# Rounding g behind its leaky step, ordering the head's first chunks by unit, and storing the last tokens by 64 columns

## The chip, the cores and the metric

The kernel runs on one core of a Trainium2 chip. Its engines work side by side, each through a queue of its own in order: TensorE (PE in the profile; its weight loads are PEld), VectorE (DVE), ScalarE (ACT), GpSimd (POOL) and SyncE (SP), which only issues DMAs here. Sixteen DMA engines move data. The metric is device time of one execution in microseconds (us).

## What is computed

```python
# attention over 32 memory slots: q, k, v (8, 8, 576, 64), phi (8, 8, 576, 32)
a = exp(phi - max(phi, axis=2)); a = a / (sum(a, axis=2) + 1e-9)
k_m = einsum('bhsm,bhsd->bhmd', a, k); v_m = einsum('bhsm,bhsd->bhmd', a, v)
scores = q @ k_m^T / 8; attn = softmax(scores)          # over the 32 slots
x = attn @ v_m                                          # (4608 tokens, 512)
# first layer
h = x @ w_in                                            # 512 -> 2048
g = maximum(0.01 * h, h)                                # the leaky step
x2 = g @ w_out                                          # 2048 -> 512
# second layer
gate = 1 / (1 + exp(-(x2 @ w_gate))); val = x2 @ w_val  # 512 -> 1536
out = (gate * val) @ w2_out                             # 1536 -> 512
```

All of it is float32. Where TensorE multiplies, the kernel writes each operand as a rounded part ("hi") and the remainder ("lo") and adds three products: hi by hi, lo by hi, hi by lo. Making the two parts, `split`, is a ScalarE cast and a subtraction on VectorE or GpSimd.

## The kernel before

**Attention and first layer.** The work goes by batch b (8), and within it by unit (b, g): g is one of two groups of four heads. A unit's chain is cut into parts: `v...` parts run on VectorE, ScalarE and GpSimd, `t...` parts on TensorE. `v10` ends the softmax, `v10t` transposes the result, `v11` splits it into `at_hi` and `at_lo`, one half of the tokens (288) after the other. x is never made: `vw` holds v_m times a block of 256 columns of w_in, per unit (`vw_block` for batch 0, `vw_pair` after), split like the rest, and h comes from `at` and `vw`.

The first layer goes by steps, one for each batch, token half `hf` and chunk `fc` of 128 of the 2048 columns (256 steps; in batch 0, groups of four chunks for one half, then for the other). A step has two parts. `m1_in` (line 845) makes h of the chunk in a bank of PSUM (`ps_h`, two banks): six products of 288 columns, three for unit g = 0 and then three for g = 1; then ScalarE's leaky step into `gr` (line 861); it hands back a function that splits `gr` into `gh` and `gl` (`ghl`). `m1_out` (line 868) adds the chunk's share of x2 to four banks `acc`: for each of four column blocks wh by gh, wl by gh, wh by gl. At a batch's end (in batch 0 at a group's end) `acc` is copied or added to `obuf` or `pbuf` and stored.

The loop over the steps (line 1373) has all engines' orders written out by hand. `LA` is 2: in iteration i come, in this order,

```python
            if fin:
                fin()                          # split of g of step i + 1
                fin = None
            if i + LA < len(steps):
                fin = step_in(*steps[i + LA])  # h and leaky step of step i + 2
```

then the other work of the iteration (units' parts, the conversion of weights by `tick`, later the preparation of the second layer's weights by `stash`, finished `vw` blocks), then `m1_out` of step i. A `tick` moves the weight pieces of w_in and w_out on by a stage each: ScalarE's `a` (y, k and the raw words), VectorE's `b` and `b2`, GpSimd's `c`, and the split `d` (ScalarE's cast of `wo`, GpSimd's subtraction). The list `gldve` names six steps whose subtraction of g is VectorE's; the others are GpSimd's.

Ahead of the loop stands the prologue, a list of groups of parts; within a group the chains of the units and of the ticks are run in turns, one piece of each in a round. After it `vw` blocks 0 and 1 are computed and split (chunks 0 and 1 need block 0, chunk 2 block 1), and `step_in` is called for steps 0 and 1.

**Second layer.** It goes by five pairs of token blocks, `PAIRS`, each of 2 h tokens, h being 512 or 384; the last has 384. Products of 2 x 2 blocks are made with seven products in place of eight. `m2_out` adds the seven products of the output weights, in the order k = 0, 2, 1, 5, 4, 3, 6, each in two column halves e, from four banks to `sums[j]`, j = 2 q + t (t: token block, q: column part); a `sum` is finished with k = 5 (j = 1), 4 (j = 3), 3 (j = 0), 6 (j = 2). `sums` hold columns on partitions, so VectorE transposes them, 32 x 32 blocks, into a tile `turned` and DMAs write rows of `out`. `turn` puts a transpose on the list `lazy`; each `read` (the VectorE or ScalarE instruction that empties a bank) takes `turns` entries from it. In the last pair's last `m2_out` (`last and end`) two entries are taken per addition, tokens are transposed by 256 and by 128, and a token block is stored when all its 512 columns have been turned: four DMAs for each of the two chunks, in pieces of 128 columns (512 B), from SyncE's and ScalarE's queues by turns.

Of the kernel before, what the change touches and what calls it, by code (L numbers as in the profile page):

```python
# [26 lines left out]
 'ticks': [1, 1, 1, 1, 2, 1, 1, 2, 0, 1, 0, 1, 1, 2, 0, 0, 0, 1, 1, 1, 1, 1, 0, 0, 1, 0, 0, 0, 0, 0],  # L27
# [95 lines left out]
def tile_kernel(  # L123
# [720 lines left out]

    def m1_in(b, hf, fc):
        p = ps_h.tile([P, 512], F32, tag="h", name="ps_h")
        t = vw[b, fc * P // VB]
        o = (fc * P) % VB
        n = 0
        for g in range(NG):  # L850
            wh, wl = t[:, 0, g, o:o + P], t[:, 1, g, o:o + P]
            i = at[b, hf, g]
            ah, al = at_hi[:, i, :], at_lo[:, i, :]
            if fc == NF - 1:
                at_free.append(i)
            for w, x in ((wh, ah), (wl, ah), (wh, al)):
                nc.tensor.matmul(p[:, :HALF], w, x, start=(n == 0), stop=(n == 3 * NG - 1))  # L857
                n += 1
        gh, gl = ghl_next()
        gr = gr_next()  # L860
# [280 lines left out]
    def m2_out(n, th, between):  # L1141
# [9 lines left out]
        def stored(t, x, m, st):  # L1151
            f = lazy.pop()
            lazy.append(lambda: (f(), store(t0 + t * h + x, m, st, end)))

        chunks = [(0, 256), (256, h - 256)]
        st = {}
        for k, e in OUT_SEQ:
# [14 lines left out]
            if th == 0 and k in (0, 2, 1, 6):  # L1172
                read(lambda: nc.scalar.copy(o, b), turns=1)
            else:
                read(lambda: nc.vector.tensor_add(o, b, o), turns=2 if end and last else 1)  # L1175
            for f in between.pop(0) if between else ():
                f()
            if last and end and (j := {5: 1, 4: 3, 3: 0, 6: 2}.get(k)) is not None:
                t = j % 2
                for x, m in chunks:  # L1180
                    if (t, x) not in st:
                        st[t, x] = turned()
                    turn(j, e, x, m, st[t, x])
                    if (k, e) in ((4, 1), (6, 1)):
                        stored(t, x, m, st[t, x])
            elif last and not end and (k, e) in ((4, 1), (6, 1)):
                t = k == 4
                for x, m in chunks:
# [4 lines left out]
                    stored(t, x, m, o)  # L1193
        while last and end and lazy:
            lazy.pop(0)()

    n_st = [0]
# [4 lines left out]

    def store(n0, m, o, end):
        for g in range(4):
            (nc.scalar if end and g % 2 else nc.sync).dma_start(
                out=out[n0:n0 + m, P * g:P * g + P].rearrange("(b p) d -> p b d", p=32),
# [4 lines left out]
    with tc.manual_schedule():  # L1211
# [114 lines left out]
        waiting = []  # L1326
        n_vw = n_in = 0
        fin = None
        for group in SCHED["prologue"]:
# [24 lines left out]
        while n_vw < 2:  # L1354
            run([first_vw(n_vw)()])
            n_vw += 1
        for i in range(LA):
            fin = step_in(*steps[i])
            if i + 1 < LA:
                fin()  # L1360

# [11 lines left out]
        for i, (b, hf, fc) in enumerate(steps):  # L1373
            if fin:
                fin()
                fin = None
            if i + LA < len(steps):
                fin = step_in(*steps[i + LA])
            else:
# [39 lines left out]
        for n in range(len(PAIRS)):  # L1419
# [25 lines left out]
            m2_out(n, NTH - 1, between)  # L1445
            if n + 2 == len(PAIRS):
                for _ in range(2):
                    t = p2[0].tile([P, 2 * PC], F32, tag="xr", name="turned", bufs=7)
                    stage2.append(t.rearrange("p (b q r) -> p b q r", q=4, r=32))

# [29 lines left out]
```

## Time and profile before

| | us |
|---|---|
| median of three runs | 1563.75 |
| lowest and highest | 1563.34 and 1563.9 |
| the profiled execution | 1563.91 |
| its span, from the first to the last instruction | 1562.1 |
| TensorE busy | 1513.7 |
| VectorE, ScalarE, GpSimd busy | 949.9, 818.4, 455.2 |

The times in the rows below are those of the profiled execution, counted from the start of its span. "Idle before" is the time in which an engine had no work ahead of an instruction, with what ended it.

### The profile page before, as it was taken

How to read it: one execution, taken by the hardware profiler on the slowest of the kernel's cores; microseconds unless marked ns; L12 is line 12 of the kernel's file. 1: busy time of each engine (PE TensorE's matmuls, PEld its weight loads, DVE VectorE, ACT ScalarE, POOL GpSimd, SP SyncE). 2: the span in 40 equal slices, each digit the busy share in tenths (PEclk: the TensorE clock that was granted, in tenths of full speed). 3: DMA queues.
4: the chain of work that ended last, by engine and by line, in shares of the span. 5: the costliest groups of instructions: out<-in, count | busy, mean ns of one | idle time of the engine just before them, and what ended most of it. 6: DMA issues, size and time to landing. Idle time of an engine off the chain costs nothing.

```text
span 1562.1 us, 28982 instructions
## 1 busy us (share of the span) xinstructions
PE 1513.7 (97%) x10508; PEld 1357.9 (87%) x10508; DVE 949.9 (61%) x1732; ACT 818.4 (52%) x1846; POOL 455.2 (29%) x445
## 2 busy tenths in 40 slices
PE   5788999999999999999999999999999999999997
PEld 2677999999999999999999988888888888889997
DVE  6886555556655555522066665757666865668567
ACT  5885565666566565644444454534532544435432
POOL 2986364554545445533200030004000210003000
PEclk9999999999999999999999999999999999999999
DMA  9822664555556555411398887667866687668875
GB/s 303 294 54 59 166 178 135 179 153 167 167 167 188 153 177 160 128 53 60 100 320 261 246 236 248 194 193 216 274 195 193 189 247 234 194 193 235 295 250 156
DMA packets 278094, 297.11 MB, mean 190 GB/s; under 512 B 102080, under 2 KB 176320, under 8 KB 277952
## 3 DMA queue, kind: packets, MB, share of 16 engines
q1 hardware_dynamic: 276288, 294.47, 63.0%
q8 instruction: 84, 1.38, 0.4%
q10 hardware_dynamic: 1664, 0.79, 0.2%
q14 instruction: 58, 0.48, 0.1%
HBM read 243.27 MB, written 51.90 MB: 189 GB/s over the span
## 4 chain that ended last, share of the span: by engine, by line
PE 79%; DVE 4%; ACT 1%; POOL 1%; issue 1%; DMA 0%; DVEq 0%; SPq 0%; ACTq 0%; POOLq 0%
PE acc L880 21%; PE ps_y L1030 18%; PE oacc L1165 13%; PE ps_h L857 10%; PE ps_z L1030 9%; PE ps_x L1030 5%; PE ps_vw L827 2%; DVE op L1046 1%; DVE sum L1175 1%; PE ps_kv L593 1%; POOL xo L953 1%; DVE sg L1049 1%; PE ps_sc L668 0%; DVE sg L1055 0%; DVE tmp L1058 0%
## 5 line engine op out<-in xcount | busy, mean ns | idle before, releaser
L880 PE MATMUL acc<-ghl,wo 128*128 128x288 f32 x3072 | 461.4, 299 | 7.3 <-ACT obuf L889 2.6
L880 PEld LDWEIGHTS acc<-ghl,wo 128*128 128x128 f32 x3072 | 420.3, 188 | 32.8 <-issue 10.7
L1030 PE MATMUL ps_y<-xo,wt 128*128 128x512 f32 (+1 forms) x1440 | 328.8, 368 | 0.0
L189 POOL TENSOR_TENSOR ghl<-grs,ghl 128x288 fp32r<-128x288 f32 x250 | 217.7, 873 | 317.7 <-ACT ghl L188 239.7
L1030 PEld LDWEIGHTS ps_y<-xo,wt 128*128 128x128 f32 x1440 | 262.5, 188 | 36.1 <-ACT tmp L1061 2.0
L1165 PE MATMUL oacc<-op,wt 128*128 128x512 f32 (+1 forms) x1260 | 265.1, 369 | 1.4 <-DVE sum L1175 0.5
L1165 PEld LDWEIGHTS oacc<-op,wt 128*128 128x128 f32 x1260 | 228.3, 188 | 35.8 <-DVE sum L1175 4.5
L861 ACT ACTIVATE grs<-ps_h 128x288 f32<-128x288 f32 x256 | 105.4, 412 | 248.7 <-PE ps_h L857 227.0
L1061 ACT COPY tmp<-ps_y 128x512 f32<-128x512 f32 (+1 forms) x180 | 98.0, 544 | 256.8 <-PE ps_y L1030 256.7
L857 PE MATMUL ps_h<-at_hi,vw 128*128 128x288 f32 x1024 | 214.1, 297 | 3.6 <-ACT vw L188 2.7
L953 POOL TENSOR_TENSOR xo<-xr,xo 128x512 fp32r<-128x512 f32 (+1 forms) x28 | 39.4, 1436 | 598.0 <-ACT xo L949 598.0
L857 PEld LDWEIGHTS ps_h<-at_hi,vw 128*128 128x128 f32 x1024 | 166.2, 190 | 5.0 <-ACT vw L188 3.6
L1030 PE MATMUL ps_z<-xo,wt 128*128 128x512 f32 (+1 forms) x720 | 167.6, 367 | 0.3 <-POOL xo L953 0.3
L1175 DVE TENSOR_TENSOR sum<-oacc,sum 128x512 f32<-128x512 f32 (+1 forms) x170 | 106.5, 633 | 89.9 <-PE oacc L1165 89.1
L857 PE MATMUL ps_h<-at_lo,vw 128*128 128x288 f32 x512 | 151.8, 297 | 0.0
L1030 PEld LDWEIGHTS ps_z<-xo,wt 128*128 128x128 f32 x720 | 131.7, 188 | 17.5 <-POOL xo L953 0.7
L1058 DVE TENSOR_TENSOR tmp<-ps_x,tmp 128x512 f32<-128x512 f32 (+1 forms) x60 | 38.0, 633 | 177.8 <-PE ps_x L1030 177.8
L1042 ACT CAST op<-sg 128x512 fp32r<-128x512 f32 (+1 forms) x180 | 103.4, 579 | 76.3 <-DVE sg L1049 47.5
L188 ACT CAST ghl<-grs 128x288 fp32r<-128x288 f32 x256 | 111.7, 436 | 1.9
L1046 DVE TENSOR_TENSOR op<-sg,op 128x512 fp32r<-128x512 f32 (+1 forms) x180 | 111.9, 645 | 0.5
L857 PEld LDWEIGHTS ps_h<-at_lo,vw 128*128 128x128 f32 x512 | 97.2, 190 | 0.0
L839 DVE TENSOR_TENSOR vw<-ps_vw,vw 128x256 fp32r<-128x256 f32 x112 | 39.7, 416 | 81.8 <-ACT vw L837 81.8
(177 smaller groups left out, 1750.0 us busy)
## 6 DMA issues: line engine op xcount, KB each, us to landing
wt<-gvs SPq DMA_DIRECT2D x420, 256.0 KB, 3.0
wt<-w2s SPq DMA_DIRECT2D x210, 256.0 KB, 3.0
gvs<-hl SPq DMA_DIRECT2D x60, 256.0 KB, 2.6
x2s<-obuf SPq DMA_DIRECT2D x15, 576.0 KB, 3.4
win<-in_moe_w_in_dram SPq DMA_DIRECT2D x16, 512.0 KB, 9.7
wo_bits<-in_moe_w_out_dram SPq DMA_DIRECT2D x16, 512.0 KB, 10.5
q<-in_q_dram SPq DMA_DIRECT2D x224, 36.0 KB, 3.0
w2s<-hl SPq DMA_DIRECT2D x30, 256.0 KB, 2.4
```

The lines of the kernel that those rows point to most:

```text
L188: nc.scalar.copy(hi, raw)
L189: eng.tensor_sub(lo, raw, f32(hi))
L857: nc.tensor.matmul(p[:, :HALF], w, x, start=(n == 0), stop=(n == 3 * NG - 1))
L861: nc.scalar.activation(gr, p[:, :HALF], AF.Prelu, alpha=0.01)
L880: nc.tensor.matmul(a[d][:, :HALF], w[:, d * P:(d + 1) * P], x, start=(open_ and n == 0), stop=(close and n == 2),)
L953: eng.tensor_sub(t[:, 1, :h], x_operand(n, k, a), f32(t[:, 0, :h]))
L1030: nc.tensor.matmul(bank, w[:, l, a, :], x[:, r, :h], start=(start and i == 0), stop=(i == 5), skip_group_check=not start,)
L1042: return lambda: nc.scalar.copy(ops[j][k][:, 0, :h], x)
L1046: return lambda: nc.vector.tensor_sub(t[:, 1, :h], x, f32(t[:, 0, :h]))
L1061: return lambda: nc.scalar.copy(d, x)
L1165: nc.tensor.matmul(b, w[:, j, l, :], ops[j][k][:, r, :h], start=(start and i == 0), stop=(i == 5), skip_group_check=not start,)
L1175: read(lambda: nc.vector.tensor_add(o, b, o), turns=2 if end and last else 1)
```

## The change

Four things are changed, and the arithmetic stays.

- In the loop, the split of a step's g is issued directly behind its leaky step, in iteration i for step i + 2, ahead of the iteration's other work; it was issued in iteration i + 1.
- The prologue's last group gets the part `v0.1`, which computes `vw` block 0 and splits it between `v10.1` and `v10t.1`; block 1 stays behind the prologue.
- Steps 0 and 1 are begun with the three products of unit 0 for both chunks; then follow the three of unit 1, leaky step and split for one chunk after the other.
- In the last pair's last `m2_out` each finished column half is transposed at once, 384 tokens in one instruction, ahead of the next addition. After the second half of a j, four DMAs store 64 columns (256 B) of 384 tokens for each group of 32 partitions. The tiles `turned` of this pair lie where `at_hi` and `at_lo`, later the second layer's `tmp`, lay, and the two further `turned` tiles of the pair before fall away. `store` of the other pairs issues from SyncE's queue alone, as it did for them.

```diff
--- before.py
+++ after.py
@@ -23,7 +23,7 @@
  'prologue': ['v1.0', 't1.0', 'v2.0 t7a.0 t2.0', 'v7a.0 v3.0', 'v3e.0 v4.0', 't7b.0 v1.1', 'T t4.0 t1.1', 'T',
               'v5.0', 'v7b.0', 'v2.1', 't5.0', 'v6.0 t2.1 t8a.0', 'T v3.1', 'v3e.1 v8a.0 t8b.0', 't7a.1', 'v8b.0',
               'v9.0 v7a.1 T v4.1 v9e.0 t4.1', 't7b.1 T', 't5.1 v5.1 v7b.1', 'T', 'v10.0 T', 't8a.1 v6.1',
-              'v10t.0 t8b.1 T v8a.1', 'v11.0', 'v8b.1 v9.1 T', 'T T v9e.1 T v10.1 v10t.1 v11.1'],
+              'v10t.0 t8b.1 T v8a.1', 'v11.0', 'v8b.1 v9.1 T', 'T T v9e.1 T v10.1 v0.1 v10t.1 v11.1'],
  'ticks': [1, 1, 1, 1, 2, 1, 1, 2, 0, 1, 0, 1, 1, 2, 0, 0, 0, 1, 1, 1, 1, 1, 0, 0, 1, 0, 0, 0, 0, 0],
  'banks': 9,
  'lopool': [0, 1, 2, 3, 4, 5, 6, 7, 8, 9, 10, 11, 12, 13, 14],
@@ -842,12 +842,12 @@
     gt = {}
     acc = {}
 
-    def m1_in(b, hf, fc):
-        p = ps_h.tile([P, 512], F32, tag="h", name="ps_h")
+    def m1_in(b, hf, fc, begun=None, gs=range(NG)):
+        p = begun or ps_h.tile([P, 512], F32, tag="h", name="ps_h")
         t = vw[b, fc * P // VB]
         o = (fc * P) % VB
-        n = 0
-        for g in range(NG):
+        n = 3 * gs[0]
+        for g in gs:
             wh, wl = t[:, 0, g, o:o + P], t[:, 1, g, o:o + P]
             i = at[b, hf, g]
             ah, al = at_hi[:, i, :], at_lo[:, i, :]
@@ -856,6 +856,8 @@
             for w, x in ((wh, ah), (wl, ah), (wh, al)):
                 nc.tensor.matmul(p[:, :HALF], w, x, start=(n == 0), stop=(n == 3 * NG - 1))
                 n += 1
+        if gs[-1] < NG - 1:
+            return p
         gh, gl = ghl_next()
         gr = gr_next()
         nc.scalar.activation(gr, p[:, :HALF], AF.Prelu, alpha=0.01)
@@ -1150,7 +1152,7 @@
 
         def stored(t, x, m, st):
             f = lazy.pop()
-            lazy.append(lambda: (f(), store(t0 + t * h + x, m, st, end)))
+            lazy.append(lambda: (f(), store(t0 + t * h + x, m, st)))
 
         chunks = [(0, 256), (256, h - 256)]
         st = {}
@@ -1172,17 +1174,23 @@
             if th == 0 and k in (0, 2, 1, 6):
                 read(lambda: nc.scalar.copy(o, b), turns=1)
             else:
-                read(lambda: nc.vector.tensor_add(o, b, o), turns=2 if end and last else 1)
+                read(lambda: nc.vector.tensor_add(o, b, o), turns=1)
             for f in between.pop(0) if between else ():
                 f()
             if last and end and (j := {5: 1, 4: 3, 3: 0, 6: 2}.get(k)) is not None:
                 t = j % 2
-                for x, m in chunks:
-                    if (t, x) not in st:
-                        st[t, x] = turned()
-                    turn(j, e, x, m, st[t, x])
-                    if (k, e) in ((4, 1), (6, 1)):
-                        stored(t, x, m, st[t, x])
+                if t not in st:
+                    st[t] = gp.tile([P, 1536], F32, tag="at_hi" if t else "at_lo", name="turned", bufs=1)
+                    st[t] = st[t].rearrange("p (b q r) -> p b q r", q=4, r=32)
+                turn(j, e, 0, h, st[t])
+                lazy.pop()()
+                if e:
+                    f = 64 * (j // 2)
+                    for g in range(4):
+                        (nc.scalar if g % 2 else nc.sync).dma_start(
+                            out=out[t0 + t * h:t0 + t * h + h, P * g + f:P * g + f + 64].rearrange("(b p) d -> p b d", p=32),
+                            in_=st[t][32 * g:32 * g + 32, :, j - t:j - t + 2].rearrange("p b q r -> p b (q r)"),
+                        )
             elif last and not end and (k, e) in ((4, 1), (6, 1)):
                 t = k == 4
                 for x, m in chunks:
@@ -1191,18 +1199,15 @@
                         for e2 in range(2):
                             turn(j, e2, x, m, o)
                     stored(t, x, m, o)
-        while last and end and lazy:
-            lazy.pop(0)()
-
     n_st = [0]
 
     def turned():
         n_st[0] += 1
         return stage2[n_st[0] % len(stage2)]
 
-    def store(n0, m, o, end):
+    def store(n0, m, o):
         for g in range(4):
-            (nc.scalar if end and g % 2 else nc.sync).dma_start(
+            nc.sync.dma_start(
                 out=out[n0:n0 + m, P * g:P * g + P].rearrange("(b p) d -> p b d", p=32),
                 in_=o[32 * g:32 * g + 32, 0:m // 32].rearrange("p b q r -> p b (q r)"),
             )
@@ -1324,8 +1329,8 @@
             else:
                 (unit_phi, unit_kv, unit_q)["pkq".index(x[0])](units[int(x[1])])
         waiting = []
-        n_vw = n_in = 0
-        fin = None
+        n_vw = 1
+        PARTS["v0"] = lambda u: first_vw(0)()
         for group in SCHED["prologue"]:
             vs, ts_ = {}, []
             for n, f in enumerate(waiting):
@@ -1354,10 +1359,9 @@
         while n_vw < 2:
             run([first_vw(n_vw)()])
             n_vw += 1
+        begun = [m1_in(*steps[i], None, (0,)) for i in range(LA)]
         for i in range(LA):
-            fin = step_in(*steps[i])
-            if i + 1 < LA:
-                fin()
+            m1_in(*steps[i], begun[i], (1,))()
 
         early = {0: [(x_open, ())] + [(x_load, (0, c)) for c in range(KD)]}
         for n in range(8):
@@ -1371,11 +1375,8 @@
         first = m2_group(0, 0, 0, 0)
         held = None
         for i, (b, hf, fc) in enumerate(steps):
-            if fin:
-                fin()
-                fin = None
             if i + LA < len(steps):
-                fin = step_in(*steps[i + LA])
+                step_in(*steps[i + LA])()
             else:
                 if not tmps:
                     tmp_open()
@@ -1443,10 +1444,6 @@
                         eng = nc.vector if len(todo) < 3 else nc.gpsimd
                         between[-1] += [lambda o=o: x_hi(*o), lambda o=o, eng=eng: x_lo(*o, eng)]
             m2_out(n, NTH - 1, between)
-            if n + 2 == len(PAIRS):
-                for _ in range(2):
-                    t = p2[0].tile([P, 2 * PC], F32, tag="xr", name="turned", bufs=7)
-                    stage2.append(t.rearrange("p (b q r) -> p b q r", q=4, r=32))
 
 
 # ---- launch: one core; inputs and outputs as the reference has them ----
```

## Rows read from the trace of the kernel before

**Rows 1.** Stretches: us, busy (x) of PE, PEld, DVE, ACT, POOL, PEclk, DMA share, GB/s

```profile
0.00:48.00 48.00, 24.28 (x162) 12.02 (x162) 32.90 (x68) 30.46 (x62) 18.38 (x21) 1.00 1.00 320
48.00:140.00 92.00, 81.21 (x683) 70.63 (x684) 73.71 (x105) 71.61 (x155) 79.96 (x64) 0.98 0.47 128
...
210.00:636.00 426.00, 424.09 (x4077) 396.72 (x4065) 249.80 (x490) 261.92 (x693) 214.67 (x223) 1.00 0.58 168
```

**Rows 2.** Time line of PE, 43 to 54: start us, us, engine, line, tiles, [idle before]

```profile
48.30 1.33 PE L857 MATMUL ps_h<-at_hi,vw 128*128 128x288 f32 x2 [2.75 <-ACT vw L188]
...
53.27 1.04 PE L880 MATMUL acc<-ghl,wo 128*128 128x288 f32 x4
```

**Rows 3.** Time line of ACT, 44 to 54 us.

```profile
44.77 0.65 ACT L218 ACTIVATE y<-wo_bits 128x512 f32<-128x512 f32 x1
...
46.48 0.43 ACT L188 CAST at_hi<-grs 128x288 fp32r<-128x288 f32 x1
...
47.67 1.06 ACT L188 CAST vw<-ps_vw 128x512 fp32r<-128x512 f32 x2
```

**Rows 4.** Time lines of DVE and of POOL, 44 to 54 us.

```profile
45.97 0.84 DVE L773 STREAM_TRANSPOSE grs<-unit_a 128x288 f32<-128x288 f32 x2 [0.88 <-POOL unit_a L758]
...
48.07 1.27 POOL L189 TENSOR_TENSOR wo<-y,wo 128x512 fp32r<-128x512 f32 x1
...
51.58 0.80 POOL L189 TENSOR_TENSOR ghl<-grs,ghl 128x288 fp32r<-128x288 f32 x1 [1.48 <-ACT ghl L188]
```

**Rows 5.** Waits of PE, 40-100, 100-130, 190-210: us in total, times, longest.

```profile
PE ps_vw L808 <- POOL win L250: 6.2, 4, 2.2
...
PE acc L880 <- POOL ghl L189: 1.3, 1, 1.3
...
PE acc L880 <- ACT ghl L188: 0.6, 1, 0.6
...
PE acc L880 <- ACT ghl L188: 1.9, 2, 1.4
PE acc L880 <- POOL ghl L189: 0.4, 1, 0.4
```

**Rows 6.** Time line of ACT, 189 to 206 us.

```profile
193.33 0.41 ACT L340 CAST sums<-sums 128x256 fp32r<-128x256 f32 x1 [2.25 <-DMA gvs<-sums]
...
194.91 0.41 ACT L188 CAST ghl<-grs 128x288 fp32r<-128x288 f32 x1
```

**Rows 7.** Waits of PE, 210-700, and time line of ACT, 384-388.

```profile
PE acc L880 <- ACT obuf L889: 0.7, 2, 0.4
...
384.54 0.41 ACT L861 ACTIVATE grs<-ps_h 128x288 f32<-128x288 f32 x1 [2.66 <-PE ps_h L857]
```

**Rows 8.** Chain of work that ended last, 1547 to 1562: start us, us, what.

```profile
1554.29 0.54 DVE turned L1147 x2
1554.83 0.44 DVE sum L1175
```

**Rows 9.** Groups by form, DVE, 1546-1562: busy us, mean ns, idle before.

```profile
L1147 DVE STREAM_TRANSPOSE turned<-sum 128x256 f32<-128x256 f32 x8 | 3.4, 422 | 0.0
L1147 DVE STREAM_TRANSPOSE turned<-sum 128x128 f32<-128x128 f32 x8 | 2.1, 268 | 0.0
```

**Rows 10.** Time lines of DVE and of SP, from 1547 us.

```profile
1547.78 1.58 DVE L1175 TENSOR_TENSOR sum<-oacc,sum 128x384 f32<-128x384 f32 x3
...
1555.19 1.14 DVE L1147 STREAM_TRANSPOSE turned<-sum 128x256 f32<-128x256 f32 x4
...
1552.70 6.36 SPq L1205 DMA_DIRECT2D out_dram<-turned  x8
```

**Rows 11.** DMA, 1552.7 to 1562.1 us: busy tenths in 40 slices, packets.

```profile
DMA  0002989979999999987899999998799950000000
...
DMA packets 3328, 1.57 MB, mean 167 GB/s; under 512 B 256, under 2 KB 3328, under 8 KB 3328
```

**Rows 12.** DMA, 4 to 6 us, mostly loads of q in 256 B pieces.

```profile
DMA packets 1755, 0.43 MB, mean 217 GB/s; under 512 B 1755, under 2 KB 1755, under 8 KB 1755
```

## The prediction

> **What bounds the kernel now.** I read the table of stretches first, since the change touches three places far apart. TensorE works 24.28 of the first 48 us, 81.21 of the next 92, and 424.09 of the 426 from 210 to 636 us [rows 1]: in the long middle it is the bound, and only its own waits can be shortened; in the head it waits. So the second view is the list of TensorE's waits by stretch, which says for whom, and the third the time lines of TensorE, ScalarE, VectorE and GpSimd around those waits. At the end TensorE isn't the bound: VectorE's chain runs to 1556.33 and the store traffic to 1560.7 [rows 10, 11], so there I read the chain of waits and the DMA view.
>
> The profiled execution took 1563.91 us (span 1562.1, so 1.8 us lie around it), 0.16 over the median 1563.75. I sum against 1563.9 and take 0.15 off at the end.
>
> **Head: order by unit, and block 0 rounded sooner.** Now chunk 0's first matmul starts at 48.30, after 2.75 us without work, released by ScalarE's cast of `vw` [rows 2]. That cast, two of them in 1.06 us from 47.67, stands behind both casts of unit 1's `at_hi` (the first at 46.48) [rows 3]. Part `v0.1` puts block 0's cast and subtraction one round ahead of unit 1's transposes, so its cast (0.53) comes in front of the `y` at 44.77 and is done at 45.3. VectorE's subtraction falls into the 0.88 us that it waits for GpSimd before 45.97 [rows 4]; what it takes beyond these would move the transposes back. TensorE can then do the six products of unit 0 for chunks 0 and 1 from 45.3 to about 47.
>
> The price: all ScalarE work behind 44.77 moves back by 0.53, and as unit 1's rounds now run one later, its first `at_hi` also falls behind a weight cast (0.5): 47.5 instead of 46.48. On GpSimd the weight subtraction (1.27, at 48.07 now [rows 4]) then goes ahead of unit 1's first `at_lo`, which ends at 49.7. Chunk 0's last product waits for it: it runs at 49.7, and at 0.24 us a product (18 of them, with their waits, fill 48.30 to 53.27 [rows 2]) chunk 1 needs one more and chunk 2 six, so that chunk 0's `m1_out` starts at 49.94 + 7 x 0.24 = 51.6, not 53.27: **1.65 us sooner on TensorE**. GpSimd's first subtraction of `g` sits at 51.58 after 1.48 us of waiting [rows 4]; with it 0.5 sooner and the next 1.25 sooner, the engines that are crowded from here on (GpSimd 79.96 and ScalarE 71.61 of 92 us [rows 1]) start 1.2 us sooner. What is passed on is the smaller: 1.0 us.
>
> **`g` rounded directly behind its leaky step.** The same instructions in another order: ScalarE's cast of chunk i+2 (and the subtraction on GpSimd or VectorE) hops over the other work of step i. It gains where that other work is held up. At 193.33 ScalarE has waited 2.25 us for a store of the stash, and only at 194.91, behind two more conversions, comes the cast for which TensorE waits [rows 6]. Between 190 and 210 us such waits are 1.9 on ScalarE's cast and 0.4 on GpSimd's subtraction; between 100 and 130 they are 0.6 and 1.3 [rows 5]. The leaky step of these chunks was over one step earlier, so all four go. The first pair I count nearly in full, **2.1 us**, as TensorE has no other wait behind it. The second pair lies where GpSimd is crowded; TensorE arrives sooner at waits for converted weights, and I keep 0.8 of the 1.9.
>
> It costs where ScalarE stands waiting for TensorE, since the other work of the step then comes one cast later (0.41 alone [rows 6], some 0.35 in a row of them). At a batch's end that other work is followed by the copies of `acc`, for which the next batch's first `m1_out` waits: 0.7 in two places, and in the one near 387 us the leaky step had waited 2.66 for TensorE [rows 7], so it can't hide. Two places by 0.35, and 0.5 as an estimate for the batch ends and unit chains that are just covered now: **+1.2 us**. On GpSimd the conversions `c` of the step now queue behind a subtraction that waits for the cast. Most of the time there is one subtraction either way; where VectorE takes one (list `gldve`), GpSimd's load moves by a step, and near 82 us a block of `vw` waits for that conversion (one of the four waits, 6.2 us together [rows 5]): one subtraction, 0.80 [rows 4], so +0.7. In the head that makes -1.0 - 0.8 + 0.7 = **-1.1 us**, with ends at -3 and +0.7. At the lower one TensorE's slow stretch goes too: the granted clock is 0.98 over these 92 us [rows 1], as if 3.7 us went at the lower of its levels (1.2 of 2.4 GHz), which costs 1.8; at the upper one the gain is lost at the next wait for weights.
>
> **Last stores.** VectorE's chain per column half is an addition of 0.44 and two transposes of together 0.54 [rows 8]. The single transpose of 384 isn't in the trace; from 422 ns for 256 and 268 for 128 [rows 9] the line gives 576, and without the second start the chain takes 0.50 (ends: 0.43 and 0.54). The addition for (5, 0) starts at 1547.78 + 0.47 = 1548.25 [rows 10]. Transposed at once, the four quarters are ready at 1550.2, 1552.1, 1554.0 and 1555.9, each with four DMAs. Now half of the output is issued from 1552.70 and the other half after VectorE's last four transposes have begun at 1555.19 [rows 10]; traffic runs from 1553.5, 0.8 after the first issue, without a pause to 1560.7: 7.1 us for 1.57 MB (the slices are 0.235 us each) [rows 11], 37 ns for each of an engine's 192 packets of 512 B. So the end is set by the traffic, and it starts 2.4 us sooner, near 1551.0.
>
> The open price is a packet of 256 B written to DRAM: the trace has none. An engine has 384 of them. The nearest row of that size is the loads of q: 1755 packets in 2 us over 16 engines [rows 12], 18.2 ns each, which makes 7.0 us, 1.75 for a quarter, less than the 1.9 between quarters, so nothing piles up. The other end is that a packet costs the 37 ns of today's stores whatever its size: 14.2 us. I take 20 ns, near the row of its size: the last quarter flows from 1555.9 + 0.8 for 1.92 us, to 1558.7 instead of 1560.6. **-1.8 us**, with -2 and +4.6 as ends. The DMAs stay 16 and stand on the same two queues; ScalarE's queue holds nothing else by then, and SyncE's weight loads are issued.
>
> The Trainium skill, "DMA: Bandwidth & Descriptors", section "Why small descriptors are slow (HBM only)", counts a packet as its bytes over 32 plus 3 cycles: 11 for 256 B against 19. By that, an estimate, 37 ns would become 21 and the term -1.7; no run so far shows it for a store.
>
> **Sum.** -1.1 (head) - 2.1 (190 to 210) + 1.2 (batch ends and unit chain) - 1.8 (end) = -3.8; 1563.9 - 3.8 - 0.15 = **1559.9 us**.
>
> **The rivals**, beside the forecast (0.49; its own range 1557 to 1562).
> *The small packets eat the gain of the last stores.* At 27 ns a quarter takes 2.6 us, more than the 1.9 between quarters, and the traffic ends at 1551.0 + 384 x 0.027 = 1561.4: +0.8 instead of -1.8, so 1562.5. For it: there are stores of 512 B that take 37 ns where loads of half the size take 18.2. Against: both carry nearly the same bytes per second (221 GB/s, 1.57 MB in 7.1 us, and 217 [rows 12]), which speaks for a limit by bytes. 0.20.
> The same page's section "Specifications" speaks against this change: it wants 512 B at least for full rate, and says that smaller transfers are done by reading, changing and writing back. No row here has such a write; full doubling is the next rival.
> *Slower: a packet costs 37 ns whatever its size.* Place: the last quarter's traffic, which then queues behind the three before it. The traffic ends at 1551.0 + 14.2 = 1565.2, 4.6 later than now, and the kernel at 1563.75 - 2.0 + 4.6 = 1566.3, slower; the end alone turns slower from 25 ns (1560.6 - 1551.0 over 384), the whole kernel from 30. 0.08.
> *The head and the middle give nothing.* The order gains for TensorE, but GpSimd and ScalarE, which set the head, only pass the wait on to the next weight block, and the batch ends cost what 190 to 210 us gives: the end's -1.8 alone, 1562.0. For it: four waits for converted weights in the head [rows 5]. 0.18.
> *The quarters wait for each other.* Both quarters of a token half lie in one tile; were the second's transpose held until the first's store has flowed (0.8 + 1.92 us, of which 0.4 are covered), once in each half, the traffic would end 4.6 later, at 1563.3, and the kernel at 1563.75 - 2.0 + 2.7 = 1564.4. Nothing in the trace shows such a hold, as the two write different columns. 0.05.
>
> **How the numbers follow.** About 0.2% (3.1 us: under 1560.6 or over 1566.9) can be told from no change. Faster by that: most of the forecast (0.38), a part of the third rival (0.06) and of the first (0.05), and the cases where TensorE's slow stretch goes, 0.03: 0.52. Slower by that: 0.05, from the second and the last. Within: 0.43. The range reaches from the forecast with the head's better end, 1556.5, to 1563.6, which takes in the first and the third rival and leaves out the two slow ones.
>
> **What would show it.** After: chunk 0's first product near 45.4 and its `m1_out` near 51.6; no wait of TensorE on `ghl` between 100 and 210 us; the waits on `obuf` near 387 and 609 us 0.3 longer; first store issued near 1550.2, last near 1556, packets of 256 B at 18 to 21 ns and traffic over by 1558.7. Wrong would be: packets of 27 ns or more, a VectorE wait between the quarters, or longer waits for weight blocks near 82 and 100 us that take back the start.

## The result, and the profile after

The changed kernel takes 1579.87 us (median of 5 runs, 1577.9 to 1584.9); the kernel before took 1563.34 beside it. The ratio is 1.011, with a 95% interval of 1.0098 to 1.0121: slower by 16.5 us, where 3.8 less were forecast. Its profiled execution took 1581.39, with a span of 1579.6.

The span grew by 17.5 us, and it can be split. The last product ends at 1572.30 instead of 1554.10 (+18.2); from there to the end are 7.3 us instead of 8.0 (-0.7). Of the 18.2, TensorE is busy 7.9 longer with the same 10508 products (1521.6 against 1513.7 on the pages), and the gaps between its products, summed, are 45.5 instead of 35.4 (+10.1). The same stretches as in [rows 1], and the four in which TensorE's granted clock is now 0.50 and before was full (columns as there):

```profile
0.00:48.00 48.00, 25.94 (x170) 13.19 (x170) 33.70 (x69) 30.36 (x61) 18.11 (x21) 0.82 1.00 320
48.00:140.00 92.00, 78.96 (x646) 68.41 (x645) 72.67 (x98) 72.60 (x153) 76.46 (x62) 0.93 0.47 128
210.00:636.00 426.00, 414.06 (x3966) 385.36 (x3965) 237.85 (x475) 269.55 (x678) 204.70 (x219) 1.00 0.55 162
...
84.35:87.76 3.41, 3.41 (x20) 2.24 (x13) 2.10 (x3) 3.00 (x8) 1.20 (x1) 0.50 0.94 120
132.14:135.55 3.41, 3.41 (x19) 2.96 (x22) 2.80 (x3) 0.97 (x3) 2.93 (x3) 0.50 0.27 39
142.38:145.79 3.41, 3.41 (x16) 3.41 (x15) 2.51 (x6) 0.28 (x1) 0.87 (x1) 0.50 0.00 0
231.12:234.53 3.41, 3.41 (x17) 3.41 (x16) 2.25 (x5) 1.33 (x3) 0.80 (x1) 0.50 0.86 242
```

In the long middle TensorE now stands still for 12 of 426 us, where it stood for 2. The four stretches run at 1.2 instead of 2.4 GHz, so each costs 1.7 us: 6.8 of the 7.9.

The 0.82 in the first row, where [rows 1] has 1.00, is not a loss. In the trace of before the record of the clock begins only at 54.03, and a stretch without a record counts as full. Its products ran at the lower level there: two of them take 0.68 us (49.67), as they do now at 51.33 in a stretch of 0.50; at the full clock they take 0.43 (49.78 now).

For whom TensorE waits from 60 to 640 us (us in total, times, longest):

```profile
PE acc L882 <- ACT obuf L891: 4.1, 5, 2.1
PE ps_vw L808 <- POOL win L250: 3.9, 2, 2.8
PE ps_kvT L638 <- ACT e L623: 3.6, 1, 3.6
PE ps_vw L827 <- DVE mx L535: 3.1, 3, 1.7
PE ps_kv L584 <- DVE t L575: 3.0, 5, 1.3
PE ps_sc L668 <- ACT kvT L650: 3.0, 2, 1.8
PE ps_sc L668 <- DVE vw L189: 1.6, 1, 1.6
...
PE acc L882 <- POOL ghl L189: 0.8, 1, 0.8
...
```

The waits for `g` itself, which the loop's part was to end [rows 5], are gone but for 0.8. In their place stand waits for the unit's own parts (`e`, `mx`, `t`, `kvT`, values on the way through the unit's chain): before, these were 0.8 in one wait, none, 0.3 and 0.8. **The other work of the step comes later.**

GpSimd's time line from 81 us, and the products that wait for it, after:

```profile
81.47 0.98 POOL L189 TENSOR_TENSOR ghl<-grs,ghl 128x288 fp32r<-128x288 f32 x1
82.42 1.70 POOL L250 TENSOR_TENSOR win<-y,k 128x512 int32<-128x512 int32 x1
...
90.37 0.81 POOL L189 TENSOR_TENSOR ghl<-grs,ghl 128x288 fp32r<-128x288 f32 x1 [4.82 <-ACT ghl L188]
91.14 1.30 POOL L250 TENSOR_TENSOR y<-y,k 128x512 int32<-128x512 int32 x1
...
84.18 1.80 PE L808 MATMUL ps_vw<-win,kvT 128*32 128x256 f32 x12 [2.78 <-POOL win L250]
...
89.09 0.29 PE L857 MATMUL ps_h<-at_lo,vw 128*128 128x288 f32 x1
```

And before:

```profile
81.36 1.50 POOL L250 TENSOR_TENSOR win<-y,k 128x512 int32<-128x512 int32 x1
...
85.77 0.84 POOL L189 TENSOR_TENSOR ghl<-grs,ghl 128x288 fp32r<-128x288 f32 x1 [0.37 <-ACT ghl L188]
86.57 1.28 POOL L250 TENSOR_TENSOR y<-y,k 128x512 int32<-128x512 int32 x1
...
82.92 1.06 PE L808 MATMUL ps_vw<-win,kvT 128*32 128x256 f32 x12 [0.96 <-POOL win L250]
```

The conversion `win` came ahead of chunk 9's subtraction (81.36; the subtraction ran at 85.77); now it comes behind it (81.47), and TensorE waits 2.78 us for it instead of 0.96. The `y` that now starts at 91.14 started at 86.57. Now GpSimd stands 4.82 us in front of chunk 11's subtraction, until TensorE has done that chunk's products (89.4), ScalarE its leaky step and its cast (from 89.86). The conversion behind needed none of these, and comes 4.6 us late. Some of that GpSimd makes good, as it had waited 2.65 us itself at 90.50; the conversion after that is 2.6 us late (93.12), and the one at 124.26 is 3.4 late (before 120.90), where TensorE is 0.4 late. TensorE gets the bill at 131 us:

```profile
128.19 0.91 DVE L189 TENSOR_TENSOR ghl<-grs,ghl 128x288 fp32r<-128x288 f32 x1 [3.10 <-ACT ghl L188]
129.02 0.15 DVE L603 TENSOR_SCALAR r<-ps_kv 128x1 f32<-128x1 f32 x1
...
128.82 0.66 ACT L218 ACTIVATE y<-wo_bits 128x512 f32<-128x512 f32 x1 [0.72 <-POOL wo L189]
...
130.49 0.46 ACT L623 ACTIVATE e<-ps_kv,r 128x256 f32<-128x256 f32 x1
...
131.01 0.44 PE L638 MATMUL ps_kvT<-ident,e 128*128 128x128 f32 x2 [3.59 <-ACT e L623]
```

ScalarE's `e` stands behind weight conversions that wait for GpSimd's, and its input `r` behind a subtraction on VectorE that waited 3.10. The same happens in the middle, from 238 us:

```profile
238.17 0.81 POOL L189 TENSOR_TENSOR ghl<-grs,ghl 128x288 fp32r<-128x288 f32 x1 [0.32 <-POOL y L250]
238.94 1.16 POOL L730 TENSOR_TENSOR e<-e,st 128x576 f32<-128x576 f32 x1
...
240.13 0.68 ACT L741 ACTIVATE e<-e 128x576 f32<-128x576 f32 x1 [2.09 <-POOL e L730]
...
240.84 0.75 DVE L747 TENSOR_REDUCE st<-e 128x18 f32<-128x576 f32 x1 [7.20 <-ACT e L741]
241.51 0.28 DVE L535 TENSOR_REDUCE mx<-ps_t 128x1 f32<-128x128 f32 x1
...
241.85 1.09 PE L827 MATMUL ps_vw<-win,kvT 64*32 64x256 f32 x30 [1.74 <-DVE mx L535]
```

GpSimd's subtraction of the unit's `e` (238.94) stands behind the one of `g`; exponential, sum and maximum follow, and TensorE waits 1.74 us for a bank of PSUM that `mx` still has to read.

To place the loss I took from each trace the start of a chunk's first `m1_out` product, less the one of before (us; the chunks count in the loop's order):

| chunk | before | whole change | loop's part | cast alone | cast, VectorE's | all but VectorE's | batches 1 to 7 | head and end |
|---|---|---|---|---|---|---|---|---|
| 0 | 53.27 | -1.22 | -0.20 | -0.62 | +0.01 | -0.13 | -0.06 | -0.85 |
| 16 | 109.64 | +2.29 | +4.32 | +1.58 | +2.32 | +2.84 | +0.00 | -0.56 |
| 20 | 124.34 | +0.38 | +2.34 | +1.15 | +1.88 | +0.91 | -0.05 | -0.54 |
| 24 | 140.16 | +5.67 | +8.61 | +1.28 | +1.82 | +7.69 | -0.01 | -0.53 |
| 40 | 185.71 | +5.72 | +8.80 | +1.30 | +1.85 | +7.81 | -0.01 | -0.54 |
| 44 | 198.00 | +4.04 | +7.19 | +0.08 | +0.17 | +6.13 | -1.69 | -1.20 |
| 48 | 210.53 | +5.12 | +8.38 | +0.21 | +0.15 | +7.32 | -0.69 | -1.21 |
| 96 | 344.25 | +13.94 | +13.78 | +1.64 | +1.45 | +13.06 | +6.27 | -1.24 |
| 252 | 762.59 | +18.11 | +17.55 | +4.30 | +3.78 | +17.20 | +10.38 | -1.80 |

The columns from "loop's part" on are the experiments below. In one profiled execution each, kernels with the same head differ by up to 0.35 at chunk 24. Between chunks 40 and 44 they differ more: there TensorE waited 1.42 us for the cast of chunk 43 before, and in other kernels with the loop as before 0.75 to 1.69.

### The profile page after: what moved, and what is told of

Read it like the earlier page. It is cut to its first block, busy times and chain, and to the rows that moved or that the text cites. A ratio compares the mean times of both kernels' runs of the same rounds, so it can differ in the third digit from the quotient of the medians.

```text
span 1579.6 us, 28933 instructions
## 1 busy us (share of the span) xinstructions
PE 1521.6 (96%) x10508; PEld 1363.5 (86%) x10508; DVE 950.0 (60%) x1724; ACT 839.2 (53%) x1846; POOL 448.9 (28%) x445
## 4 chain that ended last, share of the span: by engine, by line
PE 75%; DVE 4%; ACT 2%; issue 1%; DMA 1%; POOL 1%; SPq 0%; ACTq 0%; DVEq 0%; POOLq 0%
PE ps_y L1032 18%; PE acc L882 18%; PE oacc L1167 13%; PE ps_z L1032 9%; PE ps_h L857 9%; PE ps_x L1032 5%; PE ps_vw L827 1%; DVE sum L1177 1%; DVE op L1048 1%; PE ps_kv L593 1%; POOL xo L955 1%; DMA gvs<-sums 0%; DVE sg L1051 0%; PE ps_sc L668 0%; ACT grs L863 0%
## 5 line engine op out<-in xcount | busy, mean ns | idle before, releaser
L1032 PEld LDWEIGHTS ps_z<-xo,wt 128*128 128x128 f32 x720 | 131.7, 188 | 17.5 <-POOL xo L955 0.7
L1032 PE MATMUL ps_x<-xo,wt 128*128 128x512 f32 (+1 forms) x360 | 83.7, 367 | 0.0
## 6 DMA issues: line engine op xcount, KB each, us to landing
wo_bits<-in_moe_w_out_dram SPq DMA_DIRECT2D x16, 512.0 KB, 10.4
```

Of the source, the lines that this page charges most:

```text
L1032: nc.tensor.matmul(bank, w[:, l, a, :], x[:, r, :h], start=(start and i == 0), stop=(i == 5), skip_group_check=not start,)
```

## The experiments

The theory: what costs is the queue behind the pair (cast and subtraction), which now waits for products that TensorE has only just been given. The rivals: the new head, and the transfers.

**The loop's part alone.**

```
-                fin = step_in(*steps[i + LA])
+                step_in(*steps[i + LA])()
```

> The kernel before with the loop's part of the change alone: the cast and the subtraction of `g` for chunk i+2 directly behind its leaky step; head, prologue and last stores as before. [...] Then this part carries the whole loss: 1578 to 1583 us (before 1563.3, the whole change 1579.9), with the waits of 3.6 near 131 us, 1.8 near 230 and 1.7 near 242 us. Rival (head): the new order of the prologue brings ScalarE's and GpSimd's work out of step, which makes the 5.7 us that are lost by chunk 24; then 1572 to 1575 here. Rival (transfers): the stash's stores, for which ScalarE waits 2.73 instead of 0.91 us near 227 us, come at another time because the head is sooner; then 1570 or less here.

1580.79 us, ratio 1.0115 (1.0100 to 1.0131). This part carries the whole loss; head and transfers fall as its cause. The waits near 131 (3.71, now at 133.03) and 242 us (1.74) are there; the one expected near 230 us isn't. So the way differs: by chunk 40 this kernel is 8.8 us late and the whole change 5.7, and only the wait at 229.85 with its slow stretch brings the whole change level.

**All but the loop's part.** In the changed kernel:

```
+            if fin:
+                fin()
+                fin = None
             if i + LA < len(steps):
-                step_in(*steps[i + LA])()
+                fin = step_in(*steps[i + LA])
```

> The whole change without its loop part: head's first two chunks by unit, first weight block a round sooner, last stores by 64 columns; `g` is rounded one step later, as before. Theory (queue): with the loop as it was the loss is gone, and what is left is the head's start (1.2 us sooner at chunk 0, of which 0 to 1 last) and the end (7.3 instead of 8.0 us behind the last product): 1561.5 to 1563 us, against 1563.3. Rival (head): 1568 to 1570, with the shift of 5 us already there by chunk 24.

1562.32 us, 0.9991 (0.9982 to 1.0000), by the trace 0.5 sooner at chunk 24 and 7.2 us behind the last product. Head and last stores do give something, close to what can be told from nothing.

**Only the last stores**, the change's lines in `m2_out` and `store`:

```
+                turn(j, e, 0, h, st[t])
+                lazy.pop()()
...
+                            out=out[t0 + t * h:t0 + t * h + h, P * g + f:P * g + f + 64].rearrange("(b p) d -> p b d", p=32),
```

> Only the last stores by 64 columns, each half transposed at once; head and loop as before. By the end of the trace after (last product to end 7.3 us, before 8.0) it gives -0.5 to -0.9: 1562.4 to 1562.8. The prediction's term for this part was -1.8: 1561.5. If packets of 256 B cost as much as those of 512 B: 1566 or more.

1562.71 us against 1563.61, 0.9993 (0.9984 to 1.0002): within what was expected, and not told apart from no change by the times alone; from the last product to the end it is 7.3 us, before 8.0.

**The cast alone.** Which engine's queue? `fin[0]`, the cast, runs at once, and `fin[1]`, the subtraction, a step later.

```
-        return lambda: split(gr, gh, gl, ...)
...
+        return [lambda: nc.scalar.copy(gh, gr), lambda: eng.tensor_sub(gl, gr, f32(gh))]
...
-                fin()
+                fin[1]()
...
                 fin = step_in(*steps[i + LA])
+                fin[0]()
```

> The kernel before, with ScalarE's cast of `g` directly behind its leaky step, but the subtraction (GpSimd, for six chunks VectorE) left at its old place, one step later. It tells which engine's queue carries the loss. If GpSimd's and VectorE's (they stand before the subtraction until TensorE, leaky step and cast are through, and the unit's conversions and maxima behind it): 1562 to 1567 us. If ScalarE's (the unit's casts come behind one more cast): 1574 to 1580. If both carry a share: between.

1569.76 us, 1.0039 (1.0026 to 1.0053): between the two. The cast's share is 4 us by the trace and 6 by the medians; the other 11 come with the subtraction.

**All but VectorE's six.**

```
+                if steps[i + LA][0] or steps[i + LA][1] * NF + steps[i + LA][2] not in SCHED["gldve"]:
+                    fin()
+                    fin = None
```

> The loop's part for all chunks but the six whose subtraction VectorE takes (list `gldve`, all in the first 32 chunks); these are rounded one step later, as before. With the loop's part for all chunks TensorE is 8.6 us late by chunk 24, and near 130 us VectorE stands 3.11 us before such a subtraction, with the sums of the unit (`r`) behind it, for which ScalarE's `e` and then TensorE wait (3.7 us, and 6.8 us at the lower clock level behind it). Theory (VectorE's six subtractions make the loss of the head): the shift at chunk 24 is under 3 us and the time 1572 to 1575 (loop's part alone 1580.8). Rival (GpSimd's subtractions make it, VectorE's wait only passes it on): shift 6 us or more, 1577 or more.

1580.56 us, 1.011 (1.0097 to 1.0124), and 7.7 late at chunk 24. The theory about VectorE fell: its 3.10 us in front of `r` are real, but ScalarE's conversions, behind GpSimd's, are as late by themselves. Here `r` is ready at 125.9, and ScalarE comes to `e` only at 131.64:

```profile
129.98 0.66 ACT L218 ACTIVATE y<-wo_bits 128x512 f32<-128x512 f32 x1 [1.80 <-POOL wo L189]
...
131.64 0.46 ACT L623 ACTIVATE e<-ps_kv,r 128x256 f32<-128x256 f32 x1
```

**GpSimd's alone left late.** On top of the cast alone:

```
+        if eng is nc.vector:
+            fin = [lambda f=fin: (f[0](), f[1]()), lambda: None]
```

> The kernel before, with ScalarE's cast of `g` directly behind its leaky step for every chunk and VectorE's six subtractions directly behind it too; GpSimd's subtractions stay one step later. With the cast alone moved the time was 1569.8, with cast and all subtractions 1580.8; the six on VectorE kept back still gave 1580.6. Theory (GpSimd's subtraction is what costs the other 11 us: it waits in front of GpSimd's weight conversions for a cast of the same step, while ScalarE's next conversion waits for GpSimd): 1568 to 1572, and under 3 us late at chunk 24. Rival (either subtraction, VectorE's or GpSimd's, is enough by itself): 1575 or more.

1570.89 us, 1.0048 (1.0033 to 1.0063), 1.8 late at chunk 24, not told apart from the cast alone. So it is GpSimd's subtraction that costs the other 10 to 11 us. GpSimd's time line at the place where 4.82 us were lost:

```profile
84.19 1.39 POOL L250 TENSOR_TENSOR y<-y,k 128x512 int32<-128x512 int32 x1 [0.97 <-DVE y L242]
85.55 1.25 POOL L864 TENSOR_TENSOR ghl<-grs,ghl 128x288 fp32r<-128x288 f32 x1
86.77 1.48 POOL L250 TENSOR_TENSOR y<-y,k 128x512 int32<-128x512 int32 x1
```

The subtraction, whose inputs are a step old, starts at once, and the next `y` at 86.77, much as before (86.57).

**Batches 1 to 7 only.**

```
+                if steps[i + LA][0]:
+                    fin()
+                    fin = None
```

> The loop's part of the change for batches 1 to 7 only (chunks 32 on); the first 32 chunks, beside which the weights are converted, are rounded one step later, as before. In the trace of the loop's part alone 8.8 us are lost by chunk 32 and 8.8 behind it. Theory (the two losses are independent: in the head GpSimd's and ScalarE's weight conversions wait, later the unit's maxima and sums): 1571 to 1573.5, with no stretch at the lower clock level behind 72 us. Rival (the later waits are an echo of the head's delay, which shifts the stash's transfers against the work): under 1568.

1573.38 us, 1.0063 (1.0049 to 1.0076). Nothing is lost up to chunk 40, and 10.4 us are behind it: the middle loses without the head's delay. One thing was expected otherwise: a stretch at the lower level does come, at 234.0 us behind a wait of 1.74.

**The pair behind the unit's work** of the same step:

```
+            if fin:
+                fin()
+                fin = None
             m1_out(b, hf, fc)
```

> The kernel before, with cast and subtraction of `g` for chunk i+2 in the same step as its leaky step, but behind the unit's work of that step instead of in front of it (still ahead of the products of `m1_out` and, at a batch's end, of the copies of `acc`). Theory (queue: what costs is what stands behind the pair): without the unit's work behind it the loss is gone, but for 0.4 to 0.8 at each copy of `acc` that now waits for the pair: 1562.5 to 1566 us. Rival (the pair is too close to its leaky step, wherever it stands): 1572 or more.

1565.58 us, 1.0014 (1.0005 to 1.0023), 1.8 above its before. The pair may stand in the same step as its leaky step at a small price, if nothing of the unit is behind it. Of what is left, 0.7 are at the copies of `acc` (210 to 700 us: two waits of together 1.4 in place of the 0.7 in [rows 7]); the rest was not traced to a place:

```profile
PE acc L880 <- ACT obuf L889: 1.4, 2, 0.7
```

**Three chunks only**, on top of all but the loop's part:

```
+                if i + LA in (43, 45, 47):
+                    fin()
+                    fin = None
```

> Head's and last stores' parts of the change, and the pair directly behind the leaky step for three chunks alone, 43, 45 and 47, for which TensorE waits 0.75, 0.46 and 0.37 us in the kernel without the loop's part (1.42, 0.47 and 0.37 before). The prediction gave this place -2.1. Theory: where ScalarE's queue is held up by something other than TensorE (the store of the stash) the pair gains: 1.0 to 1.6 us less than the kernel without the loop's part, 1560.7 to 1561.3. Rival: the wait only goes to the next part of the unit, as it did in the whole change (1.6 us won by chunk 44, 1.2 lost by chunk 48): 1562 to 1563.

1561.71 us, 0.9987 (0.9979 to 0.9996), between the range of the theory and that of the rival. By the traces TensorE gains nothing against the kernel without this edit: the 0.8 us won between chunks 40 and 44 are given back by chunk 48, in waits of 0.78 for a leaky step (200.67) and 0.86 for GpSimd's `g` (203.73), where 0.46 and 0.37 stood without it. That is the rival's picture.

**Transposes one half behind.** Loop as before, new head and end; `quarter` runs the transpose and, after a second half, the four stores.

```
                 turn(j, e, 0, h, st[t])
-                lazy.pop()()
...
+                done, held_ = held_, lambda j=j, e=e, t=t, tr=lazy.pop(): quarter(j, e, t, tr)
+                if done:
+                    done()
```

> Head's and last stores' parts of the change, loop as before; of the last stores only the order of VectorE's work differs: the transpose of a half runs behind the addition of the next half, not directly behind its own. In the trace of the last stores by 64 columns an addition and the transpose that reads it start 0.55 us apart, against 0.44 where two independent ones follow each other. Theory (the transpose waits for the whole of the addition just before it): 0.10 to 0.11 less for each of seven halves, the last transposes 0.7 us sooner, and the time 1561.4 to 1561.8 against 1562.3. Rival (the transfers set the end: 384 packets of 256 B at 19.6 ns from the first quarter on): no gain, 1562.2 to 1562.8, since the first quarter is issued 0.5 us later.

1561.75 us, 0.9988 (0.9979 to 0.9997). VectorE, first as in the changed kernel, then here:

```profile
1572.31 0.58 DVE L1149 STREAM_TRANSPOSE turned<-sum 128x384 f32<-128x384 f32 x1
1572.81 0.52 DVE L1177 TENSOR_TENSOR sum<-oacc,sum 128x384 f32<-128x384 f32 x1
1573.37 0.58 DVE L1149 STREAM_TRANSPOSE turned<-sum 128x384 f32<-128x384 f32 x1
```

```profile
1552.35 0.52 DVE L1188 TENSOR_TENSOR sum<-oacc,sum 128x384 f32<-128x384 f32 x1
1552.79 0.56 DVE L1149 STREAM_TRANSPOSE turned<-sum 128x384 f32<-128x384 f32 x1
1553.27 0.52 DVE L1188 TENSOR_TENSOR sum<-oacc,sum 128x384 f32<-128x384 f32 x1
```

From addition to transpose 0.56 us where the transpose reads it, 0.44 where it doesn't; a half takes 1.06 against 0.92. VectorE ends 1.77 us behind the last product instead of 2.7, and 0.3 of that reach the end (6.9 us behind the last product, 7.2 without): the transfers take the rest. The interval overlaps that of the kernel without this edit; the 0.3 rest on the traces.

**What was left standing:** the kernel just above, and the cast alone at once for five chunks.

```
...
+                if 43 <= i + LA <= 47:
+                    fin.pop(0)()
```

> What the other runs left standing: head by unit with the first weight block a round sooner, loop as before but for ScalarE's cast alone directly behind the leaky step for chunks 43 to 47, last stores by 64 columns with the transposes one half behind. The transposes gave 0.6 (1561.75 against 1562.3). With the cast moved for every chunk and the subtraction left, 1.1 us were won between chunks 40 and 48 and kept; with both moved the same place won 1.6 and lost 1.2 by chunk 48. Theory (here ScalarE is held up by a store of the stash, and only the cast has to get past it): 1560.4 to 1561.0. Rival (no gain, as with both moved): 1561.6 to 1562.

1560.30 us against 1563.90, 0.9977 (0.9967 to 0.9986), the fastest of all, 0.1 below the range of the theory. Its trace is 0.87 ahead at chunk 24, 2.49 at chunk 44 and 2.33 at chunk 48: here the gain stays. ScalarE, where it stood before the stash [rows 6]:

```profile
187.94 0.43 ACT L866 CAST ghl<-grs 128x288 fp32r<-128x288 f32 x1
189.37 0.41 ACT L340 CAST hl<-sums 128x256 fp32r<-128x256 f32 x1 [1.00 <-DMA gvs<-hl]
192.43 0.41 ACT L340 CAST sums<-sums 128x256 fp32r<-128x256 f32 x1 [2.65 <-DMA gvs<-sums]
```

Chunk 43's cast is past the store at 187.94, not behind it at 194.91. The kernel's interval overlaps that of the one without this edit; that the 1.5 us come from here rests on the trace. How much is to be won depends on the wait that falls away: it was 1.62 us in the kernel just above (194.71), and 0.75 in the one with all but the loop's part (194.17).

## Why the prediction was wrong

**The step that failed** is the price of the loop's part. Its terms, -0.8 and -2.1 won, +0.7 and +1.2 paid, make -1.0 us; alone it measured +17.2 (1580.79 against 1563.61). What failed are the two costs: "Most of the time there is one subtraction either way", so one subtraction (0.8) near 82 us and none elsewhere, and +1.2 for batch ends and unit chains. The wait was named: "On GpSimd the conversions `c` of the step now queue behind a subtraction that waits for the cast". But I priced it by the subtraction's length, and not by how long GpSimd would then stand. On ScalarE the work of the step stood behind the leaky step already, so only one cast (0.41) came in front. GpSimd's subtraction was a step old when its turn came, and near 82 us the conversion behind ran at once. Moved up, the subtraction waits for TensorE's products, the leaky step and the cast of a chunk that has just begun, and GpSimd with it: 234.5 us of such waits from 60 to 640 us in 106 places, before 173.7 in 73.

The place near 82 us was right, its price was not: the conversion for the `vw` block comes 1.1 us later (82.42 against 81.36), about as forecast, but TensorE's wait for it grows by 1.8 us, a slow stretch follows, and the 4.82 us in front of the next subtraction had no term at all. For batches 1 to 7 the +1.2 measured +8.8 (chunks 40 to 252 of the loop's part, what is won there taken off). The waits for `obuf` at batch ends are a small part of it, 2.0 us in four places between 210 and 700 us where 1.4 in two was forecast; with the pair behind the unit's work they are 1.4 in two. Most of it is in the unit's chains, for which the 0.5 allowed too little: the waits for `mx`, `t` and `kvT` there are 6.7 us in the loop's part alone, before 1.1. The third rival had the right engines, but only as a gain that comes to nothing.

**Lost as well was the clock.** I weighed that a slow stretch might go (-1.8); four came. Of the loss about 10 us are waits and 7 the clock.

**The gains were where they were said to be, and didn't last.** The 1.9 us of waits from 100 to 130 us were won in full (chunks 16 to 20: +2.29 to +0.38; I had kept 0.8) and paid back at 131 us. Between 190 and 210 us, for -2.1, 1.6 were won and 1.1 to 1.2 of them lost by chunk 48; with the cast alone 1.1 stay (all chunks) and 1.5 (five chunks). So the mechanism was right there, for the cast. Its size is not settled: with the loop as before this place came 0.7 us sooner by itself in one trace (all but the loop's part), as its wait varies.

**Head.** After, chunk 0's first product starts at 45.28 (forecast 45.4), its last operand comes at 49.55 (49.7), `m1_out` at 52.05 (51.6), or 52.42 without the loop's part:

```profile
45.28 1.23 PE L857 MATMUL ps_h<-at_hi,vw 128*128 128x288 f32 x2
...
49.55 0.40 PE L857 MATMUL ps_h<-at_lo,vw 128*128 128x288 f32 x1 [1.30 <-POOL at_lo L189]
49.78 0.43 PE L857 MATMUL ps_h<-at_hi,vw 128*128 128x288 f32 x2
50.05 0.29 PE L857 MATMUL ps_h<-at_lo,vw 128*128 128x288 f32 x1
...
51.33 0.68 PE L857 MATMUL ps_h<-at_hi,vw 128*128 128x288 f32 x2
...
52.05 1.16 PE L882 MATMUL acc<-ghl,wo 128*128 128x288 f32 x4
```

The count was wrong: chunk 1's two other products stand behind chunk 0's last as well, nine follow and not seven, 0.5 us at the 0.24 of the forecast. (That price holds at the lower level of the clock, as at 51.33.) Instead of 1.0, 0.5 to 0.9 were passed on.

**Last stores.** -0.7 instead of -1.8. The price of the packets, the open term, held: 55.8% of 13.6 us on each engine for 384 packets of 256 B are 19.8 ns (forecast 20), against 53.2% of 12.1 us for 192 of 512 B, 33.5 ns.

```profile
q10 hardware_dynamic: 3200, 0.79, 29.1%
q1 hardware_dynamic: 3200, 0.79, 26.7%
```

What was mis-sized is VectorE's chain: 0.50 and 0.44 were taken from rows in which no instruction reads the one before it [rows 8, 9]; turned at once, each half costs 0.12 more, about 0.9 us over the eight halves, and the last quarter is ready that much later. The single transpose takes 0.56 to 0.58 (forecast 0.576). Both rivals about packets and the one about quarters fall.

By the Trainium skill, "DMA: Bandwidth & Descriptors", section "Why small descriptors are slow (HBM only)", the estimate for such a packet was 21 ns; the trace agrees, with 19.8. Its section "Specifications" has transfers under 512 B done by reading, changing and writing back: no doubling shows here, the time per byte rose by 18%.

**Two slips in the sums.** From 1560.6 to 1558.7 us are 1.9, not 1.8. And the head's better end, -3 for -1.1, makes 1558.0: the range's lower bound of 1556.5 does not come out of it. Neither decides anything, as the time lies far above.

## What to carry to other kernels

Before an instruction is moved forward in an engine's queue, ask what it waits for at its new place, and price the move by that wait for everything behind it, not by its own length. Here a subtraction whose inputs were a step old held little up; the same one fresh tied its engine to the source of its inputs. So move only the link that gets past the hold-up (here one cast, at five chunks), and leave the links on other engines a step late.

## What the runs showed of the hardware

**An instruction that reads what the one ahead of it on its engine wrote starts later.** VectorE: 0.56 instead of 0.44 us from an addition to the transpose of its result. ScalarE: 0.44 from a leaky step to its own cast (89.42 to 89.86 in the changed kernel), 0.30 from a leaky step to a copy that doesn't read it (90.02 to 90.32 without the loop's part); over 256 pairs ScalarE is busy 839.2 us instead of 818.4 with the same 1846 instructions. The Trainium skill, "VectorE: DVE Perf Modes", section "The DRAIN you can't avoid", has the next instruction start once the pipeline is empty, and sooner if it is not held; a semaphore between two cost nothing there. These rows show a difference of 0.12 us between the two cases.

**TensorE's clock fell behind some waits and not behind others.** It stood at 1.2 GHz after waits of 2.78 (84.18), 3.59 (131.01), 1.64 (141.17) and 1.78 us (229.85); after the wait of 1.74 at 241.85 it stayed at 2.4, while in the kernel with batches 1 to 7 only the same wait brought a stretch at 1.2. With the cast alone there was none from 53 us until after the last product in the profiled execution, though TensorE waited 2.48 (67.09), 2.72 (101.36) and 1.64 us (138.28), and its times spread by 3.9 us. Whether such a wait costs 1.7 us more can't be read from its length.
